# V loaded by whole batches over GpSimd's queue, with one ring of buffers for all loads

## The chip, the cores and the metric

The kernel runs on one core of a Trainium2 chip. The metric is the device time of one execution in microseconds, lower is better; runs are given by their median. The profile is one execution of its own, recorded by the hardware profiler.

## What is computed

One decode step for a batch of eight tokens: layer norm of x, attention of 32 query heads over a window of the last 2048 positions in a cache with eight key and value heads, times the SiLU of a gated unit, added to x.

```python
B, Sq, D = 8, 1, 512; Hq, Hkv, Sk, Dh = 32, 8, 8192, 128; W = 2048; F = 1792   # all bf16
xn = layernorm(x)                                    # [8, 512]
q = (xn @ wq).reshape(B, 32, 128)                    # wq [512, 4096]
k = k_cache[:, :, Sk - W:, :]                        # [8, 8, 2048, 128], each head used by 4 query heads
v = v_cache[:, :, Sk - W:, :]
p = softmax(q . k * Dh ** -0.5)                      # [8, 32, 2048]
s = (p @ v).reshape(B, 4096) @ wo                    # wo [4096, 512]
g = silu((sigmoid(xn @ w_gate) * (xn @ w_up)) @ w_down)
out = x + s * g
```

The windows of K and V are 33.6 MB each, wq and wo 4.2 MB each, the three weights of the gated unit 1.8 MB each: 81 MB are read once.

## The kernel before

**Loads.** All large loads are issued by SyncE on its one queue. `kring` has three buffers of 32 KB in each of the 128 partitions (wq, then K tiles, then the weights at the end); `vring` has four of 16 KB (V tiles). `issue_loads` (line 210) goes through one list, `loads`, in order, and stops at the first load whose buffer is not yet released in program order; the wait itself is a semaphore wait in SyncE's program. The list is sorted by slots: K tile i at slot 8i, V tile i at slot 4i + 49 (`V_LAG`), so that the order is K0 to K6, V0, V1, K7, V2 and so on; the gate and up weights go in ahead of the last two V tiles, the down weights and wo behind them. wo comes in six pieces (`load_wo`), the last ones small.

**A K tile** (`load_k`, 4 MB, eight of them) is a quarter of the window for four batches and all eight heads: 128 rows of 32 KB. **A V tile** (`load_v`, 2 MB, sixteen) is the whole window of one batch for four of its heads (`gg` is the half): 128 rows of 16 KB, a partition being (position block of 64, head).

**The slot loop** (line 657) writes the order of all engines by hand. In slot t VectorE turns an eighth of a K tile in place by 32x32 blocks (`k_turn`, line 458, 64 in all); TensorE follows four slots later with the scores of that eighth (`qk`, line 473, eight slots to a tile, 64 in all; the second half of a tile's scores needs all of its eight turns). After each K tile comes a maximum on VectorE (`soft_max_part`, line 487). After four K tiles (one set `hb` of four batches) come the exponentials on ScalarE (`soft_exp`), a turn of the probabilities (`soft_turn`), a spreading product on TensorE (`soft_spread`), and `soft_mask` (line 553): for each head of a group VectorE multiplies the probabilities by a 0/1 column `Hm`, so that each partition feeds only its own head's columns. `pv` (line 601) multiplies V with these as weights: 32 matmuls of 256 columns for a V tile in four slots, each with 32 weight columns and at four column positions, starting at slot `PV_LAG` = 52. ScalarE copies the four partial sums out (`acc_sb`, line 613), `pv_sum` (line 623) adds them with a selecting matmul and VectorE scales the result by the reciprocal of the softmax's sum (line 632).

**Buffers.** A K buffer is released when the last `qk` of its tile is done, a V buffer when the last `pv` of its tile is.

**The end.** `unit_in` (gate and up) and `unit_mid` stand in the loop shortly before its end, then the last `pv_sum`, `o_rows` (a picking product that brings the output to wo's rows), `unit_out` (the down product), 64 matmuls with wo (line 709), two VectorE steps and the output.

Of the kernel before, what the change touches and what calls it, by code (L numbers as in the profile page):

```python
# [10 lines left out]
def kernel(  # L11
# [30 lines left out]
    GL = 4  # L42
    NG = Hkv // GL
    PP = P // GL
    CH = W // PP
    NQ = P // 32
    NJ = 4
    CC = CH // NJ
    NT = B * NG
# [11 lines left out]
    VSET = NT // HB  # L61
# [4 lines left out]
    V_LAG = 49  # L66
    PV_LAG = 52
    MASK_AT = {}
    for gg in range(NG):
        MASK_AT[0, gg] = EXP_AT[0] + 9 + gg  # L70
        MASK_AT[1, gg] = max(EXP_AT[1] + 6, PV_LAG + NJ * NQ * (gg + 1))
# [3 lines left out]
    CB = CH // 2  # L75
    NCH = 2
    KRING = 3
    VRING = 4
# [15 lines left out]
    kring = ctx.enter_context(tc.tile_pool(name="kring", bufs=KRING))  # L94
    vring = ctx.enter_context(tc.tile_pool(name="vring", bufs=VRING))
    ppool = ctx.enter_context(tc.tile_pool(name="ppool", bufs=2))
# [18 lines left out]
    def k_tile(shape, name):  # L115
        return kring.tile(shape, bf16, name=name, tag="kring", align_bytes=ALIGN)

    def v_tile(shape, name):
        return vring.tile(shape, bf16, name=name, tag="vring", align_bytes=ALIGN)
# [8 lines left out]
    wq_sb = k_tile([P, KT, Hq * Dh], "wq_sb")  # L128
# [5 lines left out]
    def load_k(i):  # L134
        hb, kq = divmod(i, NK)
        t = k_tile([P, KC, Dh], "k_sb")
# [9 lines left out]
    def v_of(i):  # L146
        hb, n = divmod(i, VSET)
        gg, q = divmod(n, NQ)
        return NQ * hb + q, gg

    def load_v(i):
        b, gg = v_of(i)
        t = v_tile([P, CH, Dh], "v_sb")
        load(
            t[:].rearrange("p c d -> p (c d)"),
            A_v_cache[b, GL * gg : GL * (gg + 1), win0:Sk, :].rearrange(
                "j (p c) d -> p j (c d)", c=CH
            ),
        )
        v_tiles[i] = t  # L160
# [4 lines left out]
    def load_gate_up():  # L165
        t = k_tile([P, 2, KT, F], "wgu_sb")
        for n, w in enumerate((B_w_gate, B_w_up)):
            load(t[:, n], w.rearrange("(p kt) n -> p kt n", kt=KT))
            wgu_sb.append(t[:, n])

    def load_down():
        t = k_tile([P, FT, D], "wd_sb")
        load(t[:], B_w_down.rearrange("(p t) n -> p t n", t=FT))
        wd_sb.append(t)
# [4 lines left out]
    def load_wo():  # L179
        t = k_tile([P, KW, D], "wo_sb")  # L180
        for t0, t1 in (
            (0, 16),
            (16, 24),
            (24, 28),
            (28, 30),
            (30, 31),
            (31, 32),
        ):
            load(t[:, t0:t1, :], wo_view[:, t0:t1, :])
            for k in range(t0, t1):  # L190
                wo_parts[k] = t[:, k, :]
# [4 lines left out]
    loads = [  # L196
        (kind, i)
        for _, kind, i in sorted(
            [(KTS * i, 0, i) for i in range(NKT)]
            + [(NJ * i + V_LAG, 1, i) for i in range(NT)]  # L200
        )
    ]
# [62 lines left out]
    for c in range(NCOL):  # L265
# [32 lines left out]
    Hm = consts.tile([P, GL], f32, name="Hm")  # L298
    nc.vector.tensor_reduce(
        out=Hm[:],  # L300
        in_=ident[:].rearrange("p (a gl) -> p gl a", gl=GL),
        axis=AX.X,
# [3 lines left out]
    spread = consts.tile([P, NG, 2, PP, GL], bf16, name="spread")  # L306
    nc.gpsimd.memset(spread[:].rearrange("p a b c d -> p (a b c d)").bitcast(f32), 0.0)
    for j in range(GL):
        for gg in range(NG):
            g = NG * gg + j // 2  # L310
            nc.gpsimd.tensor_copy(
                out=spread[:, gg, j % 2, :, j], in_=ident[:, 32 * g : 32 * g + PP]
            )

    w = NCH * GL * rep
# [13 lines left out]
    pick = consts.tile([32 * NG, NE, P], bf16, name="pick")  # L329
    nc.gpsimd.memset(pick[:].rearrange("p e m -> p (e m)").bitcast(f32), 0.0)  # L330
    for gg in range(NG):
        rows = slice(32 * gg, 32 * (gg + 1))
        cols = slice(NE * GL * rep * gg, NE * GL * rep * (gg + 1))
        for e in range(NE):
            nc.gpsimd.tensor_copy(
                out=pick[rows, e, cols].rearrange("p (h d) -> p h d", d=NE)[:, :, e],
                in_=ident[rows, 32 * gg : 32 * gg + GL * rep],
            )
# [49 lines left out]


# [57 lines left out]
    o_sb = work.tile([32 * NG, B, Dh], bf16, name="o_sb")  # L447
    nc.vector.memzero(o_sb[:])
# [42 lines left out]
    def soft_exp(hb):  # L491
# [7 lines left out]
        p_bf = ppool.tile([P, CH, NK, NC, 2], bf16, name="p_bf", tag="pp")  # L499
# [25 lines left out]
    def soft_spread(hb):  # L525

        pt = pt_of.pop(hb)[:].rearrange("p c (y m) -> p c y m", y=2)
        pc = ppool.tile([P, NG, NQ, CH, rep], bf16, name="pc_bf", tag="pp")
        for gg in range(NG):
            for ch in range(2):  # L530
                c = slice(CB * ch, CB * (ch + 1))
                pT_ps = psum_a.tile([P, CB, NQ, rep], f32, name="pT_ps", tag="acc_ps")
                for y in range(2):
                    nc.tensor.matmul(  # L534
                        pT_ps[:],
                        lhsT=spread[:, gg, y].rearrange("p k g -> p (k g)"),
# [6 lines left out]
                    out=pc[:, gg, :, c, :].rearrange("p q c r -> p c q r"),  # L543
# [4 lines left out]
    def soft_mask(hb, gg):  # L548

        pT_of[hb, gg] = work2.tile([P, NQ * CB, GL, 2 * rep], bf16, name="pT_sb")  # L550
        pc = pc_of[hb][:, gg].rearrange("p q (c e) r -> p (q c) (e r)", e=2)
        for gl in range(GL):
            nc.vector.tensor_scalar(  # L553
                out=pT_of[hb, gg][:, :, gl, :],
                in0=pc,
                scalar1=Hm[:, gl : gl + 1],
# [3 lines left out]

    GW = GL * rep

    def soft_den(hb):
# [8 lines left out]
        den_ps = psum1.tile([32 * NG, NQ], f32, name="den_ps", tag="misc")  # L572
        rden = small.tile([32 * NG, NQ], f32, name="rden")
        for gg in range(NG):
            rows = slice(32 * gg, 32 * gg + GW)
            nc.tensor.matmul(
                den_ps[rows, :],
                lhsT=HR[:, GL * gg : GL * (gg + 1)].rearrange("m h r -> m (h r)"),
                rhs=dq[:],
                start=True,  # L580
                stop=True,
                tile_position=(0, 32 * gg),
                skip_group_check=True,
            )
            nc.vector.reciprocal(out=rden[rows, :], in_=den_ps[rows, :])
        rden_of[hb] = rden

    def pv(t):


        i, j = divmod(t, NJ)
        b, gg = v_of(i)
        w = GL * rep * NCH
        if j == 0:
            acc_tiles[i] = psum_a.tile([P, NCH * Dh], f32, name="acc_ps", tag="acc_ps")
        q = b % NQ
        pT = pT_of[b // NQ, gg][:, CB * q : CB * (q + 1)].rearrange("p c g n -> p (c g n)")
        for n in range(CC // NCH):
# [11 lines left out]
        if j == NJ - 1:  # L610
            if i % 2 == 0:
                acc_sbs[i // 2] = small.tile([P, 2, NCH * Dh], f32, name="acc_sb")
            nc.scalar.copy(out=acc_sbs[i // 2][:, i % 2], in_=acc_tiles.pop(i)[:])  # L613

    def pv_sum(i, n):

        b, gg = v_of(i)
        q = b % NQ
        acc_sb = acc_sbs[i // 2][:, i % 2 : i % 2 + n]
        rows = slice(32 * gg, 32 * gg + GW)  # L620
        o_ps = psum1.tile([32 * NG, 2, Dh], f32, name="o_ps", tag="misc")
# [10 lines left out]
        nc.vector.tensor_tensor(  # L632
            out=o_sb[rows, b : b + n, :],
            in0=o_ps[rows, :n, :],
            in1=rden_of[b // NQ][rows, q : q + n].unsqueeze(2).to_broadcast([GW, n, Dh]),
            op=ALU.mult,
# [20 lines left out]
    for t in range(PV_LAG + NSLOT):  # L657
# [100 lines left out]
```

## Time and profile before

| | |
|---|---|
| runs | 197.42, 197.66, 197.91 us; median 197.66 |
| the profiled execution's own time | 197.7 us |
| its span | 195.9 us |
| granted TensorE clock, mean | 0.66 |
| read from memory | 81.01 MB, 414 GB/s over the span |
| TensorE matmul / VectorE / ScalarE / GpSimd busy | 87.8 / 106.1 / 27.5 / 4.6 us |

The span is from the first to the last recorded instruction. Lines such as L458 are lines of the kernel before. A group of instructions shows line, engine, operation, output and input tiles, and the count; the waits show who waited for whom, the total, the number of times and the longest; the timeline gives start and length in us. SPq, ACTq and POOLq are the parts of SyncE, ScalarE and GpSimd that issue transfers. The granted clock is the share of TensorE's full clock that the chip allowed.

### The profile page before, as it was taken

How to read it: one execution, taken by the hardware profiler on the slowest of the kernel's cores; microseconds unless marked ns; L12 is line 12 of the kernel's file. 1: busy time of each engine (PE TensorE's matmuls, PEld its weight loads, DVE VectorE, ACT ScalarE, POOL GpSimd, SP SyncE). 2: the span in 40 equal slices, each digit the busy share in tenths (PEclk: the TensorE clock that was granted, in tenths of full speed). 3: DMA queues.
4: the chain of work that ended last, by engine and by line, in shares of the span. 5: the costliest groups of instructions: out<-in, count | busy, mean ns of one | idle time of the engine just before them, and what ended most of it. 6: DMA issues, size and time to landing. Idle time of an engine off the chain costs nothing.

```text
span 195.9 us, 2383 instructions
## 1 busy us (share of the span) xinstructions
PE 87.8 (45%) x994; PEld 39.6 (20%) x994; DVE 106.1 (54%) x152; ACT 27.5 (14%) x69; POOL 4.6 (2%) x25
## 2 busy tenths in 40 slices
PE   0007004434333248503632782856274734544683
PEld 0002001111100012100321340332132321222471
DVE  0025799999999998899969825314000000040301
ACT  2002450000000084000010051500000004000000
POOL 8000000000000000000000000000000000000000
PEclk9999755555555555555596698797655555588569
DMA  6999999999999999999999999999999999999990
GB/s 221 429 455 442 442 442 435 435 428 427 435 428 428 435 428 428 411 425 452 428 411 432 425 432 420 428 432 438 432 432 435 428 423 436 435 429 424 422 376 31
DMA packets 5002, 81.17 MB, mean 414 GB/s; under 512 B 624, under 2 KB 896, under 8 KB 1152
## 3 DMA queue, kind: packets, MB, share of 16 engines
q1 hardware_dynamic: 4912, 81.01, 96.8%
q8 instruction: 8, 0.13, 0.2%
q10 hardware_dynamic: 80, 0.01, 0.0%
q14 instruction: 2, 0.02, 0.0%
HBM read 81.01 MB, written 0.01 MB: 414 GB/s over the span
## 4 chain that ended last, share of the span: by engine, by line
DMA 66%; DVE 20%; PE 10%; issue 2%; SPq 1%; DVEq 0%
DMA k_sb<-in_A_k_cache_dram 31%; DMA v_sb<-in_A_v_cache_dram 17%; DMA wo_sb<-in_A_wo_dram 17%; DVE k_sb L458 17%; PE a_ps L709 3%; PE s_ps L473 3%; PE acc_ps L601 2%; PE pT_ps L534 1%; DVE pt_bf L521 1%; PE o_ps L623 1%; SPq L113 1%; DVE mx L487 1%; DVE qz_sb L428 0%; DVE qT_sb L418 0%; DVE prod L720 0%
## 5 line engine op out<-in xcount | busy, mean ns | idle before, releaser
L458 DVE STREAM_TRANSPOSE k_sb<-k_sb 128x1024 f32<-128x1024 f32 x64 | 73.8, 1210 | 3.2 <-DMA k_sb<-in_A_k_cache_dram 3.1
L473 PE MATMUL s_ps<-k_sb,qz_sb 128*32 128x512 bf16 x256 | 31.8, 587 | 55.2 <-DVE k_sb L458 49.4
L601 PE MATMUL acc_ps<-v_sb,pT_sb 128*32 128x256 bf16 x512 | 27.5, 340 | 22.5 <-DMA v_sb<-in_A_v_cache_dram 22.5
L632 DVE TENSOR_TENSOR o_sb<-o_ps,rden 16x256 bf16<-16x256 f32 (+1 forms) x9 | 3.5, 385 | 44.5 <-PE o_ps L623 44.4
L473 PEld LDWEIGHTS <-qz_sb 128*32 128x32 bf16 x256 | 9.5, 121 | 72.9 <-issue 47.9
L601 PEld LDWEIGHTS <-pT_sb 128*32 128x32 bf16 x512 | 15.9, 114 | 34.7 <-DMA v_sb<-in_A_v_cache_dram 26.1
L613 ACT COPY acc_sb<-acc_ps 128x256 f32<-128x256 f32 x16 | 6.0, 373 | 80.8 <-PE acc_ps L601 80.8
L623 PE MATMUL o_ps<-acc_sb,Sel 128*16 128x256 f32 (+1 forms) x36 | 13.2, 511 | 3.4 <-ACT acc_sb L613 3.4
L553 DVE TENSOR_SCALAR pT_sb<-pc_bf,Hm 128x1024 bf16<-128x1024 bf16 x16 | 6.6, 476 | 4.4 <-PE acc_ps L601 4.4
L534 PE MATMUL pT_ps<-pt_bf,spread 128*128 128x512 bf16 x16 | 7.1, 604 | 0.7 <-DVE pt_bf L521 0.7
L238 DVE CAST x_f<-x_bf 8x512 f32<-8x512 bf16 x1 | 0.4, 415 | 12.9 <-DMA x_bf<-in_A_x_dram 12.9
L261 PE MATMUL xnT_ps<-ident,xn_bf 8*128 8x8 bf16 x4 | 0.3, 175 | 15.4 <-DVE xn_bf L251 15.4
L501 ACT ACT_TABLE_LOAD x1 | 1.3, 1283 | 39.6 <-DVE nm L495 39.6
L487 DVE TENSOR_REDUCE mx<-s_ps 128x1 f32<-128x512 f32 x8 | 5.3, 662 | 1.8 <-PE s_ps L473 1.8
L521 DVE STREAM_TRANSPOSE pt_bf<-p_bf 128x512 bf16<-128x512 bf16 x8 | 4.9, 675 | 1.8 <-ACT p_bf L501 1.8
L542 ACT CAST pc_bf<-pT_ps 128x512 bf16<-128x512 f32 x8 | 4.7, 585 | 8.6 <-PE pT_ps L534 5.8
L623 PEld LDWEIGHTS o_ps<-acc_sb,Sel 128*16 128x16 f32 x36 | 3.8, 120 | 10.1 <-ACT acc_sb L613 6.0
L349 PE MATMUL d_ps<-wgu_sb,xnT_sb 128*32 128x448 bf16 x32 | 3.4, 572 | 4.9 <-DMA wgu_sb<-in_B_w_up_dram 2.5
L430 ACT COPY qz_sb<-qT_sb 32x32 bf16<-32x32 bf16 x20 | 4.8, 241 | 5.0 <-DVE qT_sb L418 4.7
L709 PE MATMUL a_ps<-wo_sb,o_sb 128*32 128x256 bf16 x64 | 5.2, 315 | 0.6 <-DMA wo_sb<-in_A_wo_dram 0.5
L501 ACT ACTIVATE p_bf<-s_ps,nm 128x512 bf16<-128x512 f32 x8 | 5.4, 685 | 0.5 <-DVE nm L495 0.5
L709 PEld LDWEIGHTS <-o_sb 128*32 128x32 bf16 x64 | 4.2, 112 | 1.9 <-issue 1.4
(59 smaller groups left out, 42.6 us busy)
## 6 DMA issues: line engine op xcount, KB each, us to landing
k_sb<-in_A_k_cache_dram SPq DMA_DIRECT2D x8, 4096.0 KB, 19.6
v_sb<-in_A_v_cache_dram SPq DMA_DIRECT2D x16, 2048.0 KB, 18.4
wq_sb<-in_A_wq_dram SPq DMA_DIRECT2D x1, 4096.0 KB, 12.5
wo_sb<-in_A_wo_dram SPq DMA_DIRECT2D x1, 2048.0 KB
wgu_sb<-in_B_w_gate_dram SPq DMA_DIRECT2D x1, 1792.0 KB
wgu_sb<-in_B_w_up_dram SPq DMA_DIRECT2D x1, 1792.0 KB
wd_sb<-in_B_w_down_dram SPq DMA_DIRECT2D x1, 1792.0 KB
wo_sb<-in_A_wo_dram SPq DMA_DIRECT2D x1, 1024.0 KB, 34.7
```

Of the source, the lines that this page charges most:

```text
L430: nc.scalar.copy(out=out, in_=in_)
L458: nc.vector.transpose(out=kw, in_=kw)
L473: nc.tensor.matmul(s_tiles[i][32 * g : 32 * (g + 1), :], lhsT=qz_sb[:, hb, h, 2 * a + e, :], rhs=kT[:, :, a, h, :, e], start=(n == 0), sto ...
L487: nc.vector.reduce_max(out=mx_of[hb][:, kq : kq + 1], in_=s_tiles[i][:], axis=AX.X)
L501: nc.scalar.activation(out=p_bf[:, :, kq], in_=s_tiles.pop(NK * hb + kq)[:].rearrange("p (o c j) -> p c j o", o=2, j=NC), func=AF.Exp, bia ...
L521: nc.vector.transpose(out=pt[:, w * n : w * (n + 1)], in_=p_bf[:, w * n : w * (n + 1)])
L534: nc.tensor.matmul(pT_ps[:], lhsT=spread[:, gg, y].rearrange("p k g -> p (k g)"), rhs=pt[:, c, y, :], start=(y == 0), stop=(y == 1), skip_ ...
L553: nc.vector.tensor_scalar(out=pT_of[hb, gg][:, :, gl, :], in0=pc, scalar1=Hm[:, gl : gl + 1], scalar2=None, op0=ALU.mult,)
L601: nc.tensor.matmul(acc_tiles[i][w * c : w * (c + 1), :], lhsT=pT[:, GL * rep * ch : GL * rep * ch + w], rhs=v_tiles[i][:, ch : ch + NCH, : ...
L613: nc.scalar.copy(out=acc_sbs[i // 2][:, i % 2], in_=acc_tiles.pop(i)[:])
L623: nc.tensor.matmul(o_ps[rows, :n, :], lhsT=Sel[:, c].rearrange("p g r -> p (g r)"), rhs=acc_sb[:, :, Dh * c : Dh * (c + 1)], start=(c == 0 ...
L709: nc.tensor.matmul(a_ps[32 * c : 32 * (c + 1), :], lhsT=o2_sb[:, k, :], rhs=wo_parts[k][:, DC * c : DC * (c + 1)], start=(k == 0), stop=(k ...
```

## The change

Every large load shares one ring of five buffers of 32 KB per partition (160 KB as before). The list of loads is wq, all eight K tiles, eight V tiles, gate and up, down, wo. wq and K stay on SyncE's queue; V and all later weights are issued by GpSimd on its own queue. A V tile is now the whole window of one batch for all eight heads, 4 MB: 128 rows of 32 KB, a partition being (quarter s of the window, head, one of four blocks of 128 positions). It is loaded by four transfers of 32 partitions, 1 MB each, in the order s = 0, 2, 1, 3.

What follows from the layout: `soft_mask` runs per batch, eight instructions of 512 elements in place of four of 1024 per group (64 instead of 16); `pv` has 64 weight columns and two column positions, and 64 matmuls in eight slots for a V tile (512 in all, as before); `spread`, `Hm`, `Sel`, `pick`, `soft_den` and `pv_sum` follow, and `o_sb` has 32 rows instead of two groups of 16. `PV_LAG` is 58, the mask of batch 0 stands at slot 52, that of batch 1 at slot 59. The gated unit's products stand behind the slot loop. `ppool` has three buffers instead of two.

In GpSimd's program the loads are its last instructions. The first transfer of a tile waits for the users of its ring buffer; besides, every transfer waits until the one eight before it on that queue has landed.

```diff
+    NJ = 8
+    NT = B
+    PV_LAG = 58
+    MASK_AT = [EXP_AT[0] + 16] + [PV_LAG + NJ * (b - 1) + 1 for b in range(1, B)]
-    KRING = 3
-    VRING = 4
+    RING = 5
+    VI = 32 // Hkv
+    VS = PP // VI
+    V_ORDER = (0, 2, 1, 3)
...
-    def load_v(i):
-        b, gg = v_of(i)
-        t = v_tile([P, CH, Dh], "v_sb")
-        load(
-            t[:].rearrange("p c d -> p (c d)"),
-            A_v_cache[b, GL * gg : GL * (gg + 1), win0:Sk, :].rearrange(
-                "j (p c) d -> p j (c d)", c=CH
-            ),
-        )
-        v_tiles[i] = t
+    def load_v(b):
+        t = ring_tile([P, CH, Dh], "v_sb")
+        for s in V_ORDER:
+            k0 = win0 + VI * CH * s
+            load(
+                t[32 * s : 32 * (s + 1)].rearrange("p c d -> p (c d)"),
+                A_v_cache[b, :, k0 : k0 + VI * CH, :].rearrange(
+                    "h (i c) d -> h i (c d)", c=CH
+                ),
+                nc.gpsimd,
+            )
+        v_tiles[b] = t
...
-            load(t[:, t0:t1, :], wo_view[:, t0:t1, :])
+            load(t[:, t0:t1, :], wo_view[:, t0:t1, :], nc.gpsimd)
...
-    loads[-2:-2] = [(2, 0)]
-    loads = loads + [(2, 1), (2, 2)]
-    k_order = [(4, 0)] + [x for x in loads if x[0] != 1]
-    v_order = [x for x in loads if x[0] == 1]
+    loads = [(0, i) for i in range(NKT)] + [(1, b) for b in range(NT)]
+    loads = loads + [(2, 0), (2, 1), (2, 2)]
+    order = [(4, 0)] + loads
...
-            order, n = (v_order, VRING) if kind == 1 else (k_order, KRING)
             at = order.index(x)
-            if at >= n and order[at - n] not in released:
+            if at >= RING and order[at - RING] not in released:
                 break
...
-    def soft_mask(hb, gg):
+    def soft_mask(b):
-        pT_of[hb, gg] = work2.tile([P, NQ * CB, GL, 2 * rep], bf16, name="pT_sb")
-        pc = pc_of[hb][:, gg].rearrange("p q (c e) r -> p (q c) (e r)", e=2)
-        for gl in range(GL):
+        pT_of[b] = work2.tile([P, CH // 2, Hkv, 2 * rep], bf16, name="pT_sb")
+        pc = pc_of[b // NQ][:, b % NQ].rearrange("p o (c e) r -> p (o c) (e r)", e=2)
+        for h in range(Hkv):
...
-        if u == NSLOT - 2 * NJ - 1:
-            unit_in(wgu_sb[0])
-            unit_in(wgu_sb[1])
-            released.add((2, 0))
-            issue_loads()
-        if u == NSLOT - 2 * NJ:
-            unit_mid()
-    pv_sum(NT - 1, 1)
+    unit_in(wgu_sb[0])
+    pv_sum(NT - 1)
+    unit_in(wgu_sb[1])
+    released.add((2, 0))
+    issue_loads()
     o_rows()
+    unit_mid()
     unit_out()
```

More of the change, by code (lines that the diff above doesn't have):

```diff
@@ L38 @@
     ALIGN = 512
-    GL = 4
-    NG = Hkv // GL
-    PP = P // GL
+    NQ = P // 32
+    PP = P // Hkv
     CH = W // PP
-    NQ = P // 32
-    NJ = 4
+    NJ = 8
     CC = CH // NJ
-    NT = B * NG
+    NT = B
     NSLOT = NT * NJ
@@ L60 @@
     SET = NK * KTS
-    VSET = NT // HB
     QK_LAG = 4
@@ L65 @@
     SPREAD_LAG = 4
[L66 to L71, printed above, removed]
+    PV_LAG = 58
+    MASK_AT = [EXP_AT[0] + 16] + [PV_LAG + NJ * (b - 1) + 1 for b in range(1, B)]
     NA = Dh // 64
-    CB = CH // 2
+    CB = CH // 4
     NCH = 2
-    KRING = 3
-    VRING = 4
+    RING = 5
+    VI = 32 // Hkv
+    VS = PP // VI
+    V_ORDER = (0, 2, 1, 3)
     NCOL = 2
@@ L93 @@
     small = ctx.enter_context(tc.tile_pool(name="small", bufs=2))
-    kring = ctx.enter_context(tc.tile_pool(name="kring", bufs=KRING))
-    vring = ctx.enter_context(tc.tile_pool(name="vring", bufs=VRING))
-    ppool = ctx.enter_context(tc.tile_pool(name="ppool", bufs=2))
+    ring = ctx.enter_context(tc.tile_pool(name="ring", bufs=RING))
+    ppool = ctx.enter_context(tc.tile_pool(name="ppool", bufs=3))
     psum = ctx.enter_context(
@@ L113, in load, with ring_tile @@
         q.dma_start(out=dst, in_=src)
[L115 to L119, printed above, removed]
+    def ring_tile(shape, name):
+        return ring.tile(shape, bf16, name=name, tag="ring", align_bytes=ALIGN)
     x_bf = work.tile([B, D], bf16, name="x_bf")
@@ L126 @@
         )
-    wq_sb = k_tile([P, KT, Hq * Dh], "wq_sb")
+    wq_sb = ring_tile([P, KT, Hq * Dh], "wq_sb")
     load(wq_sb[:], A_wq.rearrange("(p kt) n -> p kt n", kt=KT))
@@ L135, in load_k @@
         hb, kq = divmod(i, NK)
-        t = k_tile([P, KC, Dh], "k_sb")
+        t = ring_tile([P, KC, Dh], "k_sb")
         k0 = win0 + NC * KC * kq
@@ L144, in load_k @@
         k_tiles[i] = t
[L146 to L149, printed above, removed]
-    def load_v(i):
-        b, gg = v_of(i)
-        t = v_tile([P, CH, Dh], "v_sb")
-        load(
-            t[:].rearrange("p c d -> p (c d)"),
-            A_v_cache[b, GL * gg : GL * (gg + 1), win0:Sk, :].rearrange(
-                "j (p c) d -> p j (c d)", c=CH
-            ),
-        )
-        v_tiles[i] = t
+    def load_v(b):
[10 more added lines that the diff above has]
+        v_tiles[b] = t
     wgu_sb = []
@@ L165, in load_gate_up @@
     def load_gate_up():
-        t = k_tile([P, 2, KT, F], "wgu_sb")
+        t = ring_tile([P, 2, KT, F], "wgu_sb")
         for n, w in enumerate((B_w_gate, B_w_up)):
-            load(t[:, n], w.rearrange("(p kt) n -> p kt n", kt=KT))
+            load(t[:, n], w.rearrange("(p kt) n -> p kt n", kt=KT), nc.gpsimd)
             wgu_sb.append(t[:, n])
     def load_down():
-        t = k_tile([P, FT, D], "wd_sb")
-        load(t[:], B_w_down.rearrange("(p t) n -> p t n", t=FT))
+        t = ring_tile([P, FT, D], "wd_sb")
+        load(t[:], B_w_down.rearrange("(p t) n -> p t n", t=FT), nc.gpsimd)
         wd_sb.append(t)
@@ L179, in load_wo @@
     def load_wo():
-        t = k_tile([P, KW, D], "wo_sb")
+        t = ring_tile([P, KW, D], "wo_sb")
         for t0, t1 in (
@@ L188, in load_wo @@
         ):
-            load(t[:, t0:t1, :], wo_view[:, t0:t1, :])
+            load(t[:, t0:t1, :], wo_view[:, t0:t1, :], nc.gpsimd)
             for k in range(t0, t1):
                 wo_parts[k] = t[:, k, :]
[L196 to L202, printed above, removed]
-    loads[-2:-2] = [(2, 0)]
-    loads = loads + [(2, 1), (2, 2)]
-    k_order = [(4, 0)] + [x for x in loads if x[0] != 1]
-    v_order = [x for x in loads if x[0] == 1]
+    loads = [(0, i) for i in range(NKT)] + [(1, b) for b in range(NT)]
+    loads = loads + [(2, 0), (2, 1), (2, 2)]
+    order = [(4, 0)] + loads
     loads_done = [0]
@@ L296 @@
     )
-    Hm = consts.tile([P, GL], f32, name="Hm")
+    Hm = consts.tile([P, Hkv], f32, name="Hm")
     nc.vector.tensor_reduce(
         out=Hm[:],
-        in_=ident[:].rearrange("p (a gl) -> p gl a", gl=GL),
-        axis=AX.X,
+        in_=ident[:].rearrange("p (s h i) -> p h s i", s=VS, h=Hkv),
+        axis=AX.XY,
         op=ALU.add,
     )
[L306 to L310, printed above, removed]
+    spread = consts.tile([P, 2, 2, VS, Hkv // 2, 2, VI], bf16, name="spread")
+    nc.gpsimd.memset(
+        spread[:].rearrange("p o y s b e i -> p (o y s b e i)").bitcast(f32), 0.0
+    )
+    for o in range(2):
+        for y in range(2):
             nc.gpsimd.tensor_copy(
-                out=spread[:, gg, j % 2, :, j], in_=ident[:, 32 * g : 32 * g + PP]
+                out=spread[:, o, y, :, :, y, :],
+                in_=ident[:].rearrange(
+                    "p (b s i o) -> p o s b i", s=VS, i=VI, o=2
+                )[:, o],
             )
-    w = NCH * GL * rep
+    w = NCH * Hq
     rows_of = small.tile([P, w], f32, name="rows_of")
@@ L322 @@
     )
-    Sel = consts.tile([P, NCH, GL, rep], f32, name="Sel")
+    Sel = consts.tile([P, NCH, Hkv, rep], f32, name="Sel")
     nc.vector.tensor_copy(
-        out=Sel[:], in_=rows_of[:].rearrange("p (g c r) -> p c g r", g=GL, c=NCH)
+        out=Sel[:], in_=rows_of[:].rearrange("p (h c r) -> p c h r", c=NCH, r=rep)
     )
     NE = P // Hq
[L329 to L338, printed above, removed]
+    pick = consts.tile([Hq, NE, Hq, NE], bf16, name="pick")
+    nc.gpsimd.memset(pick[:].rearrange("p e h d -> p (e h d)").bitcast(f32), 0.0)
+    for e in range(NE):
+        nc.gpsimd.tensor_copy(out=pick[:, e, :, e], in_=ident[:Hq, :Hq])
     FQ = F // 4
@@ L386, in unit_out @@
         nc.vector.tensor_tensor(out=gate[:], in0=sigb[:], in1=b_ps[:], op=ALU.mult)
+    GL = P // 32
+    NG = Hkv // GL
     def q_projection():
@@ L446 @@
     acc_sbs = {}
-    o_sb = work.tile([32 * NG, B, Dh], bf16, name="o_sb")
-    nc.vector.memzero(o_sb[:])
+    o_sb = work.tile([Hq, B, Dh], bf16, name="o_sb")
     def k_turn(t):
@@ L498, in soft_exp @@
         den4 = small.tile([P, NK], f32, name="den4")
-        p_bf = ppool.tile([P, CH, NK, NC, 2], bf16, name="p_bf", tag="pp")
+        p_bf = ppool.tile([P, CH // 2, NK, NC, 2], bf16, name="p_bf", tag="pp")
         for kq in range(NK):
@@ L516, in soft_turn @@
         p_bf = p_of.pop(hb)[:].rearrange("p c k j o -> p (c k j o)")
-        pt_of[hb] = ppool.tile([P, CH, PP], bf16, name="pt_bf", tag="pp")
+        pt_of[hb] = ppool.tile([P, CH // 2, 32], bf16, name="pt_bf", tag="pp")
         pt = pt_of[hb][:].rearrange("p c m -> p (c m)")
-        w = CH * PP // 4
+        w = CH * 16 // 4
         for n in range(4):
@@ L527, in soft_spread @@
         pt = pt_of.pop(hb)[:].rearrange("p c (y m) -> p c y m", y=2)
-        pc = ppool.tile([P, NG, NQ, CH, rep], bf16, name="pc_bf", tag="pp")
-        for gg in range(NG):
+        pc = ppool.tile([P, NQ, 2, CH // 2, rep], bf16, name="pc_bf", tag="pp")
+        for o in range(2):
             for ch in range(2):
@@ L535, in soft_spread @@
                         pT_ps[:],
-                        lhsT=spread[:, gg, y].rearrange("p k g -> p (k g)"),
+                        lhsT=spread[:, o, y].rearrange("p s b e i -> p (s b e i)"),
                         rhs=pt[:, c, y, :],
@@ L542, in soft_spread @@
                 nc.scalar.copy(
-                    out=pc[:, gg, :, c, :].rearrange("p q c r -> p c q r"),
+                    out=pc[:, :, o, c, :].rearrange("p q c r -> p c q r"),
                     in_=pT_ps[:],
@@ L546, in soft_spread @@
         pc_of[hb] = pc
-    def soft_mask(hb, gg):
-        pT_of[hb, gg] = work2.tile([P, NQ * CB, GL, 2 * rep], bf16, name="pT_sb")
-        pc = pc_of[hb][:, gg].rearrange("p q (c e) r -> p (q c) (e r)", e=2)
-        for gl in range(GL):
+    def soft_mask(b):
+        pT_of[b] = work2.tile([P, CH // 2, Hkv, 2 * rep], bf16, name="pT_sb")
+        pc = pc_of[b // NQ][:, b % NQ].rearrange("p o (c e) r -> p (o c) (e r)", e=2)
+        for h in range(Hkv):
             nc.vector.tensor_scalar(
-                out=pT_of[hb, gg][:, :, gl, :],
+                out=pT_of[b][:, :, h, :],
                 in0=pc,
-                scalar1=Hm[:, gl : gl + 1],
+                scalar1=Hm[:, h : h + 1],
                 scalar2=None,
@@ L559, in soft_mask @@
             )
-    GW = GL * rep
     def soft_den(hb):
@@ L571, in soft_den @@
         )
[L572 to L585, printed above, removed]
+        den_ps = psum1.tile([Hq, NQ], f32, name="den_ps", tag="misc")
+        nc.tensor.matmul(
+            den_ps[:],
+            lhsT=HR[:].rearrange("m h r -> m (h r)"),
+            rhs=dq[:],
+            start=True,
+            stop=True,
+        )
+        rden = small.tile([Hq, NQ], f32, name="rden")
+        nc.vector.reciprocal(out=rden[:], in_=den_ps[:])
         rden_of[hb] = rden
     def pv(t):
-        i, j = divmod(t, NJ)
-        b, gg = v_of(i)
-        w = GL * rep * NCH
+        b, j = divmod(t, NJ)
+        w = NCH * Hq
         if j == 0:
-            acc_tiles[i] = psum_a.tile([P, NCH * Dh], f32, name="acc_ps", tag="acc_ps")
-        q = b % NQ
-        pT = pT_of[b // NQ, gg][:, CB * q : CB * (q + 1)].rearrange("p c g n -> p (c g n)")
+            acc_tiles[b] = psum_a.tile([P, NCH * Dh], f32, name="acc_ps", tag="acc_ps")
         for n in range(CC // NCH):
@@ L601, in pv @@
             nc.tensor.matmul(
-                acc_tiles[i][w * c : w * (c + 1), :],
-                lhsT=pT[:, GL * rep * ch : GL * rep * ch + w],
-                rhs=v_tiles[i][:, ch : ch + NCH, :].rearrange("p c d -> p (c d)"),
+                acc_tiles[b][w * c : w * (c + 1), :],
+                lhsT=pT_of[b][:, ch // NCH].rearrange("p h n -> p (h n)"),
+                rhs=v_tiles[b][:, ch : ch + NCH, :].rearrange("p c d -> p (c d)"),
                 start=(j == 0 and n < P // w),
@@ L610, in pv, with pv_sum @@
         if j == NJ - 1:
[L611 to L621, printed above, removed]
+            acc_sbs[b] = small.tile([P, NCH * Dh], f32, name="acc_sb")
+            nc.scalar.copy(out=acc_sbs[b][:], in_=acc_tiles.pop(b)[:])
+    def pv_sum(b):
+        acc_sb = acc_sbs.pop(b)
+        o_ps = psum1.tile([Hq, Dh], f32, name="o_ps", tag="misc")
         for c in range(NCH):
             nc.tensor.matmul(
-                o_ps[rows, :n, :],
-                lhsT=Sel[:, c].rearrange("p g r -> p (g r)"),
-                rhs=acc_sb[:, :, Dh * c : Dh * (c + 1)],
+                o_ps[:],
+                lhsT=Sel[:, c].rearrange("p h r -> p (h r)"),
+                rhs=acc_sb[:, Dh * c : Dh * (c + 1)],
                 start=(c == 0),
                 stop=(c == NCH - 1),
-                tile_position=(0, 32 * gg),
-                skip_group_check=True,
-            )
[L632 to L636, printed above, removed]
+            )
+        nc.vector.tensor_scalar(
+            out=o_sb[:, b, :],
+            in0=o_ps[:],
+            scalar1=rden_of[b // NQ][:, b % NQ : b % NQ + 1],
+            scalar2=None,
+            op0=ALU.mult,
         )
@@ L646, in o_rows @@
                 o2_ps[:],
-                lhsT=pick[:, e, :],
+                lhsT=pick[:, e].rearrange("p h d -> p (h d)"),
                 rhs=o_sb[:, :, KW * e : KW * (e + 1)],
@@ L663 @@
                 soft_exp(hb)
-            for gg in range(NG):
-                if t == MASK_AT[hb, gg]:
-                    soft_mask(hb, gg)
+        for b in range(B):
+            if t == MASK_AT[b]:
+                soft_mask(b)
         if t < KSLOT:
@@ L675 @@
             qk(t - QK_LAG)
-        if u >= NJ and u % NJ == 0:
-            i = u // NJ - 1
-            if i == NT - 2:
-                pv_sum(i, 1)
-            elif i % 2 == 1:
-                pv_sum(i - 1, 2)
+        if u >= NJ and u % NJ == 2:
+            pv_sum(u // NJ - 1)
         if u >= 0:
```

## The prediction

> **What bounds the kernel now.** I read the page's slices and DMA queues first, then the chain that ended last, then SyncE's and VectorE's timelines around the step from K to V.
>
> ```profile
> DMA  6999999999999999999999999999999999999990
> GB/s 221 429 455 442 442 442 435 435 428 427 435 428 428 435 428 428 411 425 452 428 411 432 425 432 420 428 432 438 432 432 435 428 423 436 435 429 424 422 376 31
> q1 hardware_dynamic: 4912, 81.01, 96.8%
> ```
>
> All 16 DMA engines are busy from slice 1 to slice 38, and one queue, SyncE's, holds 96.8% of their span: 189.6 of 195.9 us. The bytes do not change, so only two things can move the end: what a byte costs, and any idle time. The packet records of the trace give the first: a 32 KB packet takes 1.213 us and a 16 KB one 0.611 us (medians). So 32 KB rows are only 0.7% cheaper. A 4 MB tile is 128 rows of 32 KB, eight for each engine: 9.70 us.
>
> ```profile
> DMA 66%; DVE 20%; PE 10%; issue 2%; SPq 1%; DVEq 0%
> 1.19 21.65 DMA k_sb<-in_A_k_cache_dram
> 35.48 17.55 DMA k_sb<-in_A_k_cache_dram
> ```
>
> The chain runs through transfers. K0 lands at 22.84 and K3 at 53.03, 30.2 us for three tiles of 9.70: from there on the last engine is 1.1 us behind.
>
> ```profile
> 1.19 64.19 SPq L113 DMA_DIRECT2D k_sb<-in_A_k_cache_dram  x7
> 80.05 0.54 SPq L113 DMA_DIRECT2D k_sb<-in_A_k_cache_dram  x1
> 58.24 9.17 DVE L458 STREAM_TRANSPOSE k_sb<-k_sb 128x1024 f32<-128x1024 f32 x8
> 101.67 4.63 DVE L458 STREAM_TRANSPOSE k_sb<-k_sb 128x1024 f32<-128x1024 f32 x4 [1.91 <-DMA k_sb<-in_A_k_cache_dram]
> 83.53 1.63 DVE L553 TENSOR_SCALAR pT_sb<-pc_bf,Hm 128x1024 bf16<-128x1024 bf16 x4
> DVE x_f L238 <- DMA x_bf<-in_A_x_dram: 12.9, 1, 12.9
> ```
>
> The columns of the first five are start, length, engine and line. The seventh K load (K6) needs K3's buffer and is issued at about 64.8 (its issue ends at 65.38): that is when K3 has been used. VectorE turns a K tile in 9.2 us plus 0.6 for the maximum, as fast as it arrives, so a late K tile can't be made up. The last line matters most: x comes in four 2 KB pieces on ScalarE's own queue, issued by 2.5 us, and the last lands at 12.9. The packet records show why. Beside q1 every small packet of q10 waits for one 32 KB packet of q1: they stand at 6.0, 7.2, 8.4, 9.7, 10.9 and 12.1. Two queues with work are served in turn, packet by packet.
>
> **What goes and comes on the transfers.** V: 2048 rows of 16 KB become 1024 of 32 KB, per engine 128 x 0.611 = 78.2 us against 64 x 1.213 = 77.6: **0.6 us less**. K, wq and the weights keep their rows. Splitting a tile into four transfers adds 16 net (16 to 32), each with one closing packet of 9 ns per engine: 0.1 us, nothing. Without idle time the end is 0.6 us earlier.
>
> **The other engines.** VectorE's masks: 16 of 128x1024 (0.39 us apart, from 1.63 for four) become 64 of 128x512. Halving the part that grows with length gives about 0.26 each, 2.05 per batch (bounds 1.6 and 3.1), 16 us against 6.5 in all. Batches 2 to 7 fall where VectorE idles (2.8 of 25 us busy from 130 to 155); batches 0 and 1 stand among the turns of K6 and K7 and count below. TensorE's V products stay 512 of 256 columns, but only two run side by side with 64-column weights where four did: 32 took 1.06 to 1.90 us, so 64 for 4 MB take 4.2 to 7.6, below the 9.70 of a tile's arrival: hidden. The 16 accumulator copies become eight, and the row sums and reciprocals halve: all off the chain. GpSimd's constant copies fall from 16 to 8 before any load needs it; its loads are last in its program, so nothing is queued behind a waiting load but later loads. At the end V7 lands about 22 us before the last byte instead of 14. The down and output weights behind it take 4.3 and 10.0 us, so the up projection's land at about 178.3 (192.5 less 14.3) and it needs 1.7; pick products, cast, gate product and turn (1.0, 1.3, 0.6, 1.0) and 3.2 us for the down projection bring the last matmuls to about 187.4, where they begin today (187.51). Nothing gained there, 0.5 lost at most.
>
> **The step from K to V.** Here I expect the loss. The ring is wq, K0..K7, V0..V7, then the weights, five buffers: V0 needs K3's, V1 K4's, V4 needs K7's. On paper V is behind all of K; but it is on another queue, and V0 may go as soon as K3 is used, while half of K5 and all of K6 and K7 still stand in SyncE's queue. Served in turn, K gets half the rate.
> - V0's first packet: 64.8 plus the issue. SyncE's first load took 1.0 us from issue (0.74) to packet (1.75); GpSimd's path is not in this trace. I take 1.2: 66.0. A slower path lets K run alone longer but delays V4 by as much, so this term cancels.
> - K7 alone would land at 22.84 + 7 x 9.70 + 1.1 = 91.8, some 0.5 of it after the last byte. At 66.0 that leaves 25.3 us of work; in turn with V0, V1 and V2 (whose buffers are free by about 76 and 92, before the queue reaches them at 85 and 105) it takes 50.6: K7 lands at 117, not 92, and K6 at about 98.
> - VectorE waits for K6 and again for K7. K7's eight turns, one maximum and batch 1's mask: 9.2 + 0.6 + 2.05 = 11.8, to 128.8. TensorE's last four score steps and the V products between them, some 2.1 us at full clock (0.21 a score step as at 112.6, twice that a V step), 4.2 at half: 130.9 to 133.
> - V4 can then go: first packet at 132.1 with the lower of these and 1.2.
> - What is in the queues by then is 13 tiles, through V3; the last engine finishes them at 22.84 + 11 x 9.70 + 1.1 - 0.5 = 130.1.
>
> So the engines run dry for **2.0 us** counted on the last engine, the one that sets the end. V4's four transfers are issued one by one, so the second half of the engines may start later: 0.5. V5 needs V0's products, over with K7's: no second gap. The range of this term: 0 if masks and matmuls take the low ends and K3 is used 1 us later (each us there is one off the gap); 4.5 with the half clock and masks at 3.1.
>
> **Sum**, against the profiled execution (197.7, span 195.9, 1.8 around it; median of the runs 197.66, so the same): 197.7 - 0.6 + 2.0 + 0.5 = **199.6 us**. With the ends of the gap, 197.1 to 202.
>
> **Rivals.**
> 1. *The gap is covered.* V4 decides: if its first packet goes out before 130 no engine idles, and only the cheaper rows are left: 197.1, at the edge of what can be told (about 0.3%, 0.6 us). For it: 2 us is little after six estimates, and if the queues are not served evenly, K having more than half, K7 lands sooner (at 60% of the turns 25.3 us become 42, 8 less). Against: x's packets, one for one.
> 2. *A transfer of 32 partitions does not reach all of the path.* No row here has that shape; the nearest, x's 8 rows, shows eight packets and eight closing ones for each piece, so eight engines. [...]
> 3. *GpSimd's packets cost more.* V and weights are 100 us of engine time; descriptors made by software are not in the trace. If a row were cut into 4 KB packets (0.159 us each in this trace), 32 KB would take 1.27, 5% more: 4 to 5 us, near 202 with a covered gap and 204 with the open one. At no extra cost it is the forecast.
>
> **How the numbers follow.** Forecast 0.52 (a gap of 1 to 4.5 us, 198 to 202), covered gap 0.27 (196.7 to 198.2), half paths 0.08, dear packets 0.13. The range 196.8 to 203 holds the first two and half of the last. Faster by over 0.3% (below 197.07) is most of half of rival 1: 0.15. Within 0.3%: the rest of it and a short gap, 0.15. Slower: 0.70.
>
> **What would show it.** Right: V0 issued at 65, K6 and K7 landing near 98 and 117, VectorE idle before both, and a dip in the GB/s row near slice 27 while the DMA digits are 9 elsewhere. Wrong: K7 landing near 92, or V4's issue before 130 with DMA at 9 throughout. V tiles landing 19 us apart after K is done would be rival 2, and 32 KB packets above 1.213 us on GpSimd's queue rival 3.

## The result, and the profile after

The changed kernel takes 197.99 us (median of 20 runs, 197.70 to 198.67) against 197.51 before (20 runs, 197.32 to 197.91): a ratio of 1.0027, interval 1.0019 to 1.0035. That is 0.5 us slower, where 2 us were forecast. The profiled execution took 197.94 us, its span 196.1.

The page of the changed kernel, slices and queues:

```profile
DMA  6999999999999999999999999999999999999990
GB/s 214 429 428 448 435 461 448 430 435 438 421 428 428 435 428 428 428 425 428 428 435 428 428 428 425 428 430 425 448 418 435 430 430 431 401 433 432 420 387 34
DMA packets 5004, 81.19 MB, mean 414 GB/s; under 512 B 1904, under 2 KB 1920, under 8 KB 2176
q0 software_dynamic: 3600, 43.26, 51.8%
q1 hardware_dynamic: 1312, 37.75, 45.0%
```

There is no dip near slice 27: the gap did not come. Half of the time is now on q0, GpSimd's queue. The third line holds what I had not counted: 1904 packets under 512 B, against 624 before.

The step from K to V, from the chain that ended last (K7's landing), the timelines of GpSimd, VectorE and TensorE, and the waits (the last two lines: who waited for whom, us in total, times, longest):

```profile
65.31 2.33 POOL L107 DMA_DIRECT2D v_sb<-in_A_v_cache_dram  x4 [61.05 <-PE s_ps L452]
54.56 47.13 DMA k_sb<-in_A_k_cache_dram
87.56 4.62 DVE L437 STREAM_TRANSPOSE k_sb<-k_sb 128x1024 f32<-128x1024 f32 x4 [1.16 <-DMA k_sb<-in_A_k_cache_dram]
101.72 3.50 DVE L437 STREAM_TRANSPOSE k_sb<-k_sb 128x1024 f32<-128x1024 f32 x3 [2.33 <-DMA k_sb<-in_A_k_cache_dram]
115.48 0.63 PE L570 MATMUL acc_ps<-v_sb,pT_sb 128*64 128x256 bf16 x8
116.41 1.06 POOL L107 DMA_DIRECT2D v_sb<-in_A_v_cache_dram  x2 [4.16 <-PE acc_ps L570]
116.92 0.40 PE L452 MATMUL s_ps<-k_sb,qz_sb 128*32 128x512 bf16 x4
DVE k_sb L437 <- DMA k_sb<-in_A_k_cache_dram: 5.3, 4, 2.3
PE acc_ps L570 <- DMA v_sb<-in_A_v_cache_dram: 16.5, 5, 4.1
```

V0 is issued at 65.3 as said. K6 lands at 87.5 and K7 at 101.7: later than alone (91.8 for K7 in the prediction's working), far earlier than the 117 of one-for-one service. VectorE waits for K 5.3 us in all. V4 is issued at 116.4, when the last products with V0 (the TensorE line at 115.48) are done. The last two of V3's four pieces land at 130.1 and 130.9, so V4 has 13.7 us to spare. K7's last scores (the line at 116.92) end at 117.3.

### The profile page after: what moved, and what is told of

The parts are those of the page before. It is cut to its first block, busy times and chain, and to the rows that moved or that the text cites. A ratio compares the mean times of both kernels' runs of the same rounds, so it can differ in the third digit from the quotient of the medians.

```text
span 196.1 us, 2425 instructions
## 1 busy us (share of the span) xinstructions
PE 95.0 (48%) x986; PEld 52.4 (27%) x986; DVE 114.5 (58%) x196; ACT 24.6 (13%) x61; POOL 25.5 (13%) x58
## 2 busy tenths in 40 slices
DMA packets 5004, 81.19 MB, mean 414 GB/s; under 512 B 1904, under 2 KB 1920, under 8 KB 2176
## 4 chain that ended last, share of the span: by engine, by line
DMA 68%; DVE 22%; PE 6%; ACT 1%; issue 1%; POOL 0%; SPq 0%; POOLq 0%; ACTq 0%
DMA k_sb<-in_A_k_cache_dram 35%; DMA v_sb<-in_A_v_cache_dram 20%; DVE k_sb L437 16%; DMA wo_sb<-in_A_wo_dram 13%; PE s_ps L452 2%; PE acc_ps L570 2%; DVE pT_sb L532 2%; ACT p_bf L480 1%; DVE pt_bf L500 1%; DVE mx L466 1%; PE a_ps L666 1%; PE pT_ps L513 1%; DVE qz_sb L408 0%; DVE qT_sb L398 0%; POOL wo_sb L107 0%
## 5 line engine op out<-in xcount | busy, mean ns | idle before, releaser
L452 PE MATMUL s_ps<-k_sb,qz_sb 128*32 128x512 bf16 x256 | 30.2, 591 | 55.5 <-DVE k_sb L437 49.7
L570 PE MATMUL acc_ps<-v_sb,pT_sb 128*64 128x256 bf16 x512 | 38.0, 304 | 16.5 <-DMA v_sb<-in_A_v_cache_dram 16.5
L570 PEld LDWEIGHTS <-pT_sb 128*64 128x64 bf16 x512 | 29.5, 122 | 25.4 <-issue 24.2
L107 POOL DMA_DIRECT2D v_sb<-in_A_v_cache_dram x32 | 17.2, 542 | 130.0 <-PE s_ps L452 80.0
L532 DVE TENSOR_SCALAR pT_sb<-pc_bf,Hm 128x512 bf16<-128x512 bf16 x64 | 17.5, 345 | 12.5 <-PE acc_ps L570 12.5
L594 DVE TENSOR_SCALAR o_sb<-o_ps,rden 32x128 bf16<-32x128 f32 x8 | 2.7, 336 | 24.8 <-PE o_ps L587 24.8
L581 ACT COPY acc_sb<-acc_ps 128x256 f32<-128x256 f32 x8 | 3.0, 372 | 81.7 <-PE acc_ps L570 81.7
L240 PE MATMUL xnT_ps<-ident,xn_bf 8*128 8x8 bf16 x4 | 0.3, 175 | 15.6 <-DVE xn_bf L230 15.6
L587 PE MATMUL o_ps<-acc_sb,Sel 128*32 128x128 f32 x32 | 6.3, 331 | 0.0
L107 POOL DMA_DIRECT2D wo_sb<-in_A_wo_dram x6 | 3.2, 535 | 10.5 <-DMA v_sb<-in_A_v_cache_dram 7.4
L352 PE MATMUL b_ps<-wd_sb,hT_sb 128*32 128x256 bf16 x28 | 3.2, 418 | 2.8 <-DVE hT_sb L344 2.8
## 6 DMA issues: line engine op xcount, KB each, us to landing
v_sb<-in_A_v_cache_dram POOLq DMA_DIRECT2D x32, 1024.0 KB, 19.5
```

Of the source, the lines that this page charges most:

```text
L107: q.dma_start(out=dst, in_=src)
L452: nc.tensor.matmul(s_tiles[i][32 * g : 32 * (g + 1), :], lhsT=qz_sb[:, hb, h, 2 * a + e, :], rhs=kT[:, :, a, h, :, e], start=(n == 0), sto ...
L532: nc.vector.tensor_scalar(out=pT_of[b][:, :, h, :], in0=pc, scalar1=Hm[:, h : h + 1], scalar2=None, op0=ALU.mult,)
L570: nc.tensor.matmul(acc_tiles[b][w * c : w * (c + 1), :], lhsT=pT_of[b][:, ch // NCH].rearrange("p h n -> p (h n)"), rhs=v_tiles[b][:, ch : ...
L587: nc.tensor.matmul(o_ps[:], lhsT=Sel[:, c].rearrange("p h r -> p (h r)"), rhs=acc_sb[:, Dh * c : Dh * (c + 1)], start=(c == 0), stop=(c == ...
```

## The experiments

In the packet records of the changed kernel, q0 holds 1680 packets of 4 B. The nine weight transfers, on 16 engines each, account for 16 apiece; each of the 32 V transfers has 48. Where packets that follow each other without a break are strung together into engines, four 32 KB packets of V are followed by six of 4 B, with a whole K packet between any two: one closing packet, and five from the next transfer, which by this reading has its data on the other eight engines. So V has 20 turns per tile and engine of which 8 carry data; K, whose turns all carry data, keeps 20 parts of 28. Between 69 and 99 us 270 packets of K started and 128 of V: 68%.

Theory A: these empty turns (the 4 B packets) held V back, so K7 came early and the gap was covered; the same packets cost time once K is done. Rival B: the share comes from how the two kinds of queue are served. Rival C: software descriptors cost per byte.

**One transfer per tile, GpSimd's queue.**

```diff
-        for s in V_ORDER:
-            ...
+        load(
+            t[:].rearrange("p c d -> p (c d)"),
+            A_v_cache[b, :, win0:Sk, :].rearrange("h (i c) d -> i h (c d)", c=CH),
+            nc.gpsimd,
+        )
...
```

(the lines of `Hm` and `spread` that follow the new order of partitions are left out here)

> A V tile comes in one transfer of 128 partitions (block of 128 positions, head) on GpSimd's queue instead of four of 32; masks and spreading matrix follow the new order of partitions, the sums are the same. Theory A (the tiny packets of the half that carries no data take turns against K's packets, so K keeps 20 turns of 28, and they cost 12 x 9 ns per engine and tile): without them K and V are served one for one, K6 lands near 94 and K7 near 114 instead of 101.7; V4 is issued near 128 instead of 116.4, at the edge of the data's end at 130, so a gap of 0 to 3 us; after K the V tiles land 9.69 us apart instead of 9.79. Time 197.2 with no gap, up to 200. Rival B (the share of K comes from how the two kinds of queue are served, not from the tiny packets): K7 still lands near 102, V4 issued near 116, no gap. Rival C (software descriptors cost per byte, not per tiny packet): V tiles still 9.79 apart, time 198.

297.4 us (six runs, 293.0 to 305.3), half as long again as before. No theory had this. V's 32 KB packets took 2.50 us (median) instead of 1.213, on all 16 engines.

**The same on SyncE's queue.**

```diff
-            nc.gpsimd,
```

(against the run above; the weights likewise)

> The same tiles and the same single transfer per V tile, but all loads on SyncE's queue, K ahead of V in one line. Theory A: K7 lands near 92, V4 issued near 108 or when the queue lets it, no gap, V tiles 9.69 us apart as K tiles are: 197.0, below before (197.5) by 0.5 and below the changed kernel (198.0) by 1.0. Rival C: the same, so e1 against e2 tells C from A. If V tiles stay at 9.79 here, neither the queue nor the tiny packets cost it, and it is the reading of V.

279.9 us. The slices of this run, V alone from about slice 13:

```profile
GB/s 299 448 429 429 415 444 441 434 429 420 438 443 380 200 224 214 191 210 207 219 224 211 205 189 219 224 210 219 207 200 205 224 220 210 217 190 412 426 393 28
```

Half rate while the DMA digits stay at 9: busy engines, packets of about 2.5 us. So it is not the queue. The two runs say nothing of A, B or C.

**Eight transfers of 16 partitions.**

```diff
-    VI = 32 // Hkv
-    V_ORDER = (0, 2, 1, 3)
+    VI = 16 // Hkv
+    V_ORDER = (0, 4, 1, 5, 2, 6, 3, 7)
...
-                t[32 * s : 32 * (s + 1)].rearrange("p c d -> p (c d)"),
+                t[16 * s : 16 * (s + 1)].rearrange("p c d -> p (c d)"),
```

> A V tile in eight transfers of 16 partitions on GpSimd's queue, halves still in turn: twice the tiny packets, the same 32 KB rows. Theory A: 96 more closing and empty packets of 4 B in each tile than four transfers have 192 of, so 24 x 9 ns per engine and tile instead of 12: V tiles 9.90 us apart after K, 0.9 us more in all, 198.9; and during the overlap V gets 8 turns of 40 instead of 8 of 28, so K7 lands nearer 97 than 101.7. Rival C: no change in the 9.79. Rival B: K7 stays at 102.

294.1 us, V packets of 2.37 us: the same, and the dose of empty packets is drowned in it. The dose was also smaller than expected: each of these transfers has 32 packets of 4 B on q0, not 48, so 64 more in a tile and not 96.

**Order 0, 1, 2, 3.**

```diff
-    V_ORDER = (0, 2, 1, 3)
+    V_ORDER = (0, 1, 2, 3)
```

> The changed kernel with the four transfers of a V tile in the order 0, 1, 2, 3. If the engines of a transfer are chosen in turn, eight and the next eight, both halves of the engines now write partitions 0 to 63 and then 64 to 127 at the same time. [...]

286.3 us, V packets of 2.53 us. Slices, and the V line of the transfers (KB each, median us from issue to landing; 19.5 in the changed kernel):

```profile
GB/s 295 442 441 442 428 420 416 442 428 437 340 235 228 239 239 354 271 216 202 209 202 213 207 219 221 207 202 212 207 214 212 216 222 213 205 184 380 432 419 86
v_sb<-in_A_v_cache_dram POOLq DMA_DIRECT2D x32, 1024.0 KB, 39.3
```

The bytes, the rows, the queue and the number of transfers are the same; what has changed is which quarters of a tile move side by side. If neighbouring transfers use opposite halves of the engines, as the packet records suggest, partitions 0 to 31 beside 32 to 63 ran at half rate here (2.53 us a packet), 0 to 31 beside 64 to 95 at full rate (1.213 us in the changed kernel). Why one pairing is slower is not shown. One rival was not tested by itself: the quarters that are read from memory side by side change with the order too, 128 KB apart in each head instead of 256. Against it speaks the run before this one, which also reads 256 KB apart and runs at half rate. For the two single-transfer runs and the one with 16 partitions (2.50, about 2.5 and 2.37 us a packet) the author's guess at the cause is the same, partitions written side by side in a slow pairing: which engine writes which partition is not in the trace.

**One transfer with K's pattern of rows, GpSimd's queue.** K's transfers run at full rate on all engines (packets of 1.213 us, DMA digits of 9), so V borrows their pattern.

```diff
+        hb, kq = divmod(b, NK)
+        k0 = win0 + NC * KC * kq
+        load(
+            t[:].rearrange("p c d -> p (c d)"),
+            A_v_cache[NQ * hb : NQ * (hb + 1), :, k0 : k0 + NC * KC, :].rearrange(
+                "b h (j c) d -> (b h) j (c d)", c=KC
+            ),
+            nc.gpsimd,
+        )
```

> The changed kernel, but each V tile is one transfer of 128 partitions on GpSimd's queue with K's pattern of rows (four batches, eight heads, a quarter of the window, 32 KB each), so that all 16 engines carry data and none of a transfer is empty. V tiles then hold V rows in another order, so the attention sum is another one; every instruction is as before. Theory A (the empty turns of the half without data give K 20 turns of 28 in the changed kernel, and cost 12 x 9 ns per engine and tile): now K and V share one for one from 69 on, K6 lands near 94, K7 near 114 instead of 101.7, V4 is issued near 128 (K7 + 14.7 as in the changed kernel), its packets near 131, the data end near 130: an idle gap of 0 to 3 us; V tiles after K 9.70 us apart instead of 9.79. Time 197.2 without a gap, up to 200 with it. Rival B (the share follows from the two kinds of queue): K7 still near 102. Rival C (software descriptors cost per byte): V tiles 9.79 apart.

201.04 us, ratio 1.0179 (1.0166 to 1.0192). The count of packets and the slices, then VectorE's and GpSimd's timelines, then a window of the stretch around 130 us (busy us of five engines with counts, clock, DMA share, GB/s):

```profile
DMA packets 3595, 81.18 MB, mean 408 GB/s; under 512 B 496, under 2 KB 512, under 8 KB 768
DMA  7999999999999999999999999789999999999980
GB/s 251 442 442 435 422 435 422 422 417 438 468 435 435 422 428 428 422 418 435 474 435 428 422 435 428 339 296 428 430 425 418 428 430 438 403 424 426 424 362 12
95.64 4.62 DVE L437 STREAM_TRANSPOSE k_sb<-k_sb 128x1024 f32<-128x1024 f32 x4 [8.80 <-DMA k_sb<-in_A_k_cache_dram]
114.96 3.50 DVE L437 STREAM_TRANSPOSE k_sb<-k_sb 128x1024 f32<-128x1024 f32 x3 [7.49 <-DMA k_sb<-in_A_k_cache_dram]
129.21 0.53 POOL L107 DMA_DIRECT2D v_sb<-in_A_v_cache_dram  x1 [17.83 <-PE acc_ps L570]
130.43 0.56 POOL L107 DMA_DIRECT2D v_sb<-in_A_v_cache_dram  x1 [0.70 <-PE s_ps L452]
126.00:133.00 7.00, 7.00 (x102) 4.51 (x100) 4.13 (x13) 1.16 (x4) 1.09 (x2) 1.00 0.74 274
```

Here K and V share the engines as the prediction assumed. With no empty turns (q0 has 16 packets of 4 B per transfer) K and V are served one for one: 272 packets of K and 285 of V from 69 to 111 us. K6 lands at 95.6, K7 at 114.9 (117 forecast), V4, the fifth V load, is issued at 129.2 and V5 at 130.4. The engines run dry: a share of 0.74 over 7 us is 1.8 us. By the packet records most of them stop at 128.5 and the last at 130.3, and V4's first packet starts at 130.4, 1.2 us after its issue. So the gap has the forecast size, 2 us, though the times around it are not quite the forecast ones (130.1 for the data's end, 132.1 for V4's first packet). The whole kernel is 3.5 us slower than before, not 2: the last packet from memory ends 2.4 us later (194.6 against 192.2), the output is issued 3.0 later (196.6 against 193.6), and this rest was not taken apart. B falls: the queues are the same two. C falls too: from 116 to 126 us, V alone, the bytes that lie in the window (each packet by its part) give 9.681 us for 4 MB, the rate of K's tiles (9.69 in the changed kernel from 50 to 64 us). (After the gap V runs at 9.80 in this kernel, from 145 to 153 us, with some packets longer than 1.25 us; why is not shown.)

**The same on SyncE's queue.**

```diff
-            nc.gpsimd,
```

(and the weights likewise)

> The same as the run with K's pattern of rows on GpSimd's queue (V rows in another order, another attention sum), but all loads on SyncE's queue, K ahead of V. All theories: K7 lands near 92, no gap, V tiles 9.69 apart: 197.0 against 197.5 before, the most that 32 KB rows can bring. If it is 197.5, the rows bring nothing and the loss of the changed kernel is all of 0.5; if V tiles are 19 us apart, the doubling seen with single transfers comes from V's memory and not from the order of partitions.

197.72 us, ratio 1.0017 (1.0000 to 1.0034), 12 runs from 197.24 to 199.2. No gap, V at 9.682 us per 4 MB from 96 to 112. So 32 KB rows without any drawback bring no gain that the runs can show; the best of its runs, 197.24, is as fast as the best of before beside it, 197.25.

**Eight transfers of half rows.** Each V transfer of 32 partitions is cut in two along the row.

```diff
-        for s in V_ORDER:
-            k0 = win0 + VI * CH * s
+        for f in range(2):
+            for s in V_ORDER:
...
+                    t[32 * s : 32 * (s + 1), CH // 2 * f : CH // 2 * (f + 1)].rearrange(
```

> The changed kernel with each V tile in eight transfers of 32 partitions and 16 KB rows, halves of the engines still in turn: twice the transfers and twice the empty and closing packets (24 per engine and tile), the sums are the reference's. Theory A: V tiles after K 9.75 + 0.22 = 9.97 us apart, 1.4 us more over eight tiles: 199.4; while K is in its queue V has 16 half packets of 40 turns, K keeps 40 of 48 units of time, so K7 lands near 97 instead of 101.7. Rival C: 9.8 to 9.85, 198.3. Rival B: K7 near 102.

199.02 us, ratio 1.0076 (1.0063 to 1.0089). K7 lands at 96.7 (97 said by A), earlier than with half as many empty packets. But this half of the run does not tell A from B: V's data packets are doubled as well, so six empty ones still follow four with data, K still has 270 packets to V's 124 (from 69 to 94 us), and K7 comes sooner because each V packet is half as long. The dose shows once K is done: 9.89 us for a V tile from 105 to 135 (9.97 said) against 9.78 in the changed kernel in the same stretch. That is 0.11 us for 12 more small packets per engine, 0.108 at 9 ns each; some 0.04 of it is the price of 16 KB rows (below). The direction is A's, the size somewhat less.

**Four transfers on SyncE's queue.**

```diff
-                nc.gpsimd,
             )
         v_tiles[b] = t
```

> The changed kernel with V's four transfers of 32 partitions per tile issued on SyncE's queue instead of GpSimd's; the weights stay on GpSimd's. If this queue gives every transfer of eight leading rows to the same eight engines, V moves at half rate: tiles 19.4 us apart, about 275. If it moves on by eight as GpSimd's queue seems to, or spreads over 16, 198 or less.

301.9 us. The DMA digits tell why:

```profile
DMA  8999999999995444455444469649654796544100
GB/s 312 457 425 421 421 435 449 438 425 421 421 436 237 210 210 213 215 224 228 212 213 210 215 257 351 212 203 243 213 220 215 277 320 213 216 210 209 49 2 3
```

From slice 12 on half of the engines are busy (8.0 of 16 by the records from 100 to 170 us), V tiles 19.3 us apart, V's packets at 1.213 us each. So from SyncE's queue these transfers keep 8 engines busy, from GpSimd's queue the same transfers kept all 16 (DMA digits of 9 in the changed kernel). Which eight serve here is not visible.

No run here points to a version faster than the kernel before.

## Why the prediction was right or wrong

- *All 16 engines are busy, only idle time or dearer bytes can move the end:* right, in every run.
- *V0 goes at 65, long before K is in, and the queues are served in turn:* right. The first V packet came at 69.2, 3.9 us after the issue instead of 1.2. That this term cancels is not borne out: in the run with K's rows on GpSimd's queue V0 took 3.7 us and V4 1.2, so K ran alone longer and V4 was not late by as much. With 13.7 us to spare it does not matter here.
- *"In turn with V0, V1 and V2 it takes 50.6":* **the step that failed.** It counted only V's data packets as turns. 12 of V's 20 turns per tile are 4 B long, K kept 68% rather than half, and K7 landed at 101.7, not 117. The run without empty turns gave 114.9 and the gap.
- *From K7's landing to its last use, 11.8 + 2.1 to 4.2:* right: 101.7 to 117.3, 15.6 us. Eight masks took 2.15 us (2.05).
- *V4 needs K7's buffer:* not quite. V4's issue follows V0's last product, which stands just ahead of K7's last scores, in both kernels with an early V (116.1 and 116.4 us here; in the run with K's rows V4 goes at 129.2 behind a product, V5 at 130.4 behind a score). This is worth about 1 us and changes nothing here.
- *The data end at 130.1:* right, V3's last two pieces landed at 130.1 and 130.9. So V4 had 13.7 us to spare and the 2.0 + 0.5 of the sum fell away: rival 1, with the mechanism it named, K having more than half (68%). No run shows the 0.5, half of the engines starting later on V4: V0's four issues took 2.33 us together, and in the run with the gap V4 was one transfer.
- *Rows: "0.6 us less".* Too much. It came from packet durations, and packets overlap (16 of 0.611 us add up to 9.78 and 8 of 1.213 to 9.70 per engine and tile): with V alone, in windows without an instruction fetch (q8 in the queues), 4 MB take 9.725 us in 16 KB rows (before, 130 to 139) and 9.682 in 32 KB rows on SyncE's queue. Eight tiles: 0.34 us.
- *Splitting: "one closing packet of 9 ns per engine: 0.1 us, nothing".* Wrong by 48 packets for 16: 9.745 us per tile (changed kernel, 104 to 118) against 9.681 with one transfer on the same queue: 0.5 us over eight tiles. It takes back the rows' gain and 0.2 more. Other stretches without a fetch give 9.72 to 9.76 before, 9.74 to 9.79 in the changed kernel and 9.68 to 9.71 for 32 KB rows on SyncE's queue, so these differences hold to about 0.04 us a tile.
- *Hidden edits:* right. The V products took 3.68 us a tile at a granted clock of 1.00 (64 from 129.73), under 9.7; the last matmuls began at 187.6 (187.4 said, 187.5 before).
- *Rival 2, half paths:* not in this order of transfers, but two runs with transfers of 32 partitions show half rate: 286 us with the order 0, 1, 2, 3 (all engines busy, packets of 2.53 us) and 302 on SyncE's queue (8.0 of 16 engines busy, packets of 1.213). Half rate for V is 77.6 us more by an estimate, 64 packets of 1.213 us per engine taking twice as long; the two cost 89 and 104. The order 0, 2, 1, 3 is what keeps the rate: 4 MB in 9.745 us is 430 GB/s, against about 210 in the order 0, 1, 2, 3. *Rival 3:* no, packets on GpSimd's queue take 1.213 us.
- What stays open: the 0.5 us between the medians. V's rate should cost 0.2 of it, but in the two profiles the last packet from memory ends together, at 192.17 and at 192.21 before, so something else makes up for it there. What the profiles do show is a longer close: from the end of the output's last packet to the end of the span 1.46 us, against 1.32 before. In every run with loads on GpSimd's queue it is 1.44 to 1.72 us, in the two others with SyncE's alone 1.31 and 1.32. That is 0.14 us; the rest has no place in these traces.

## What to carry to other kernels

Where two queues carry loads at the same time, count the packets on each, the 4 B ones too: in these traces service goes by packets (K 270 to V's 128 with 12 of V's 20 turns empty, 272 to 285 with none), so small ones push their own stream back, and what looks like an order of loads in the program is none between queues. A load that goes early can delay the one whose buffer a later load waits for; with even service the kernel took 3 us more than the changed one, 2 of them idle, and only the empty packets hid it. And when a tile is cut into partition blocks, check the time of a single packet first: another order of the same blocks doubled it here (2.53 us against 1.213).

## What the runs showed of the hardware that was not expected

- With transfers of 32 partitions in the order 0, 1, 2, 3 a 32 KB packet took 2.53 us, in the order 0, 2, 1, 3 1.213 us, at 430 GB/s in all. That neighbours run side by side, to partitions 0 to 31 and 32 to 63 or to 0 to 31 and 64 to 95, is inferred. A V tile in one transfer of 128 partitions on GpSimd's queue ran at half rate too (2.50 us a packet), with K's pattern of rows at full rate (4 MB in 9.681 us).
- On GpSimd's queue a V transfer of 32 partitions (eight heads, four rows of 32 KB each) has 48 packets of 4 B; with eight closing ones taken off, that is five for each of the eight engines that, by the strung records, carry none of its data. With two rows a head (16 partitions) there are 32 per transfer, which makes three. On SyncE's queue the same transfers leave the eight closing ones alone: 408 packets of 4 B there, 16 for each of nine loads, 8 for each of 32 V transfers and 8 for the output.
- The time from GpSimd's issue to the first V packet was 3.9 us beside a full queue, against 1.0 for SyncE's first load on idle engines. For V4 in the run with K's rows, with most engines dry, it was 1.2.
- The runs with loads on GpSimd's queue closed 0.12 to 0.41 us later behind their last output packet than those on SyncE's queue alone (1.44 to 1.72 against 1.31 to 1.32 us).
